# Two Fourier transforms and two feed-forward layers on one core: the start of the kernel rearranged, and the order in which a block leaves its accumulators

## The chip, the core and the metric

The kernel runs on one core of a Trainium2 chip. The time is the device time of one execution in microseconds; before the change it was 970.33 us, the median of three runs (968.51, 970.33 and 970.53 us). Engines are named as in the profile: PE (TensorE matmul) with PEld (its weight loads), DVE (VectorE), ACT (ScalarE), POOL (GpSimd) and SP, which issues nearly all transfers.

## The reference, cut to what matters

```
X = np.fft.fft(x, axis=1); X = np.fft.fft(X, axis=2); x = X.real.reshape(6016, 256)
h = x @ w_in;   g = np.maximum(h, 0) + alpha * np.minimum(h, 0);   x = g @ w_out     # 2048 wide
h = x @ w_in2;  g = h * (1 / (1 + np.exp(-h)));                    out = g @ w_out2  # 2048 wide
```

x is (2, 3008, 256) in f32. The weights arrive as 64-bit floating-point words and are narrowed to f32 on the chip.

## The kernel before, in words

The sequence of 3008 is taken as 47 times 64. Stage A transforms the 47, stage B the 64; the transform over the 256 features is not run on the data but multiplied into `w_in` once ("mixing", `mix_w`). The token columns are cut into NC = 6 blocks `c` of 8 rows by 64 columns, the 2048 hidden units into NF = 16 groups `m` of 128. Products that need f32 accuracy are made from a high part in a reduced f32 format and a low part (the rest): three matmuls of 512 columns stand for one.

**The front** (lines 887 to 993). `spin` issues ten dummy matmuls on zeros. The first image's x is loaded in eight pieces `x0`, of eight rows each, between raw weights (512 KB each); `stage_u` takes eight rows at a time, two matmul records a row, and ACT and DVE in turn copy the result into `u_all`. Between the units the first two input weights (`first[0]`, `first[1]`) and the first output weight (`wo0`) are narrowed and the first two are mixed. Then come stage B of block 0 (`psB`, line 976), one matmul that spreads a row over all partitions (`psP`, line 989) and its copies `pb` (991).

**First layer** (line 1030 on). Step (c, m) is `step1`: two groups of three matmuls into `psh` (line 578, three PSUM banks with tag "h"), then on DVE h (586), the sum (587) and the difference (589), on ACT two Relus (588, 590), on DVE two `r` (592). A bank is free for a later step when its `r` is done. `close1` splits r into `gh` (ACT, 608) and `gl` (POOL, 609) and queues `second1`: eight matmuls with gh and four with gl into four `pso` banks (624). It is pulled two steps later, eight in the first half of that step and four in the second. After the twelve matmuls of a block's last m, `save_x2` copies the four `pso` banks out, two on ACT (635) and two on DVE (636), and the next block uses the same four banks.

**Side work.** `at(step, job)` starts a job (a generator) at a step; it goes on at phases of the steps (`EARLY`, `BANK`, `AMID`, `MID1`, `MID2`, `LATE`). `win` narrows and mixes an input weight (ACT 227 and 228, DVE 233 and 235, PE 534, DVE 549 for the low part, then the `column` sums on PE, 540). `narrow_wout` narrows an output weight and ends with its high part on ACT (279) and its low part on POOL (280); pair n is first used by `second1(0, 2n)`. For the output weights with no raw tile of their own the load is issued at the named step and the narrowing follows two steps later. `back_stage_a` is stage A of the second image, `stage_b` the stage B of later blocks, four per block, and `rank_one(c)` computes a block's spread row, writes it to DRAM (480) and reads it back to all partitions as `pb[c]` (491). It waits for the four `stage_b` of its block; the read is issued two steps after the matmul. A block's first h (586) needs `pb[c]`. All steps are constants: `NARROW`, `WOUT`, `STAGE_A`, `STAGE_B`.

**Second layer** (line 1045 on). Same pattern with seven products per pair (744), sums (765) and second products (812); the change touches it in one line.

SP issues transfers in the order of the program and waits at each for the data it needs.

Of the kernel before, what the change touches and what calls it, by code (L numbers as in the profile page):

```python
# [97 lines left out]
def kernel(  # L98
# [422 lines left out]
    def mix_w(p, pool=None, tag="x"):  # L521
# [22 lines left out]

        if p < 2:

            column(pool.tile([P, 2, 2], F32, name="psS", tag=tag))
        yield BANK
        V.tensor_tensor(lo, ps, f32(hi), op=ALU.subtract)
        mixed.add(p)  # L550
        if p > 1:
            yield EARLY
            yield from claim()
            column(ptile([P, 2, 2], "psS"))

    def win(p, convert):
# [6 lines left out]
    def step1(c, m):  # L563
# [22 lines left out]
        V.scalar_tensor_tensor(t[:, :w], pb[c][:, :w], wst[:, m, 0:1], ps[0][:, :w], op0=ALU.mult, op1=ALU.add)  # L586
        V.tensor_tensor(ps[0][:, :w], t[:, :w], ps[1][:, :w], op=ALU.add)  # L587
        A.activation(r[:, 0, :w], ps[0][:, :w], AF.Relu, scale=-1.0)  # L588
        V.tensor_tensor(ps[1][:, :w], t[:, :w], ps[1][:, :w], op=ALU.subtract)  # L589
# [22 lines left out]
    def second1(c, m, hi, lo):  # L612
# [7 lines left out]
        for passes in (((0, hi), (1, hi)), ((0, lo),)):  # L620
            for s in range(2):
                for k in range(2):
                    for a, g in passes:
                        T.matmul(po[c][s][k][:, :w], wo1[q][:, mm, a, k * P:(k + 1) * P], g[:, s, :w],  # L624
                                 start=m == 0 and a == 0 and g is hi, stop=m == NF - 1 and g is lo)
                        n += 1
                        if n == 12 and m == NF - 1:
                            save_x2(c)
                        yield

    def save_x2(c):
# [217 lines left out]
    def start_win2():  # L849
# [20 lines left out]
    STEP2 = [0] + [NC * NF + 56 * c for c in range(NC - 1)]  # L870
    SPIN = 10,

    BEHIND = {2: ("i", 0), 4: ("i", 1), 7: ("o", 0)}
    UNITS = 8, 8, 8, 8, 8, 8, 8, 4, 4
    AMONG = {0: ((0, 1),), 1: ((0, 5),), 2: ((1, 1),), 3: ((1, 5),), 4: ((2, 1),), 8: ((2, 4),)}
    RAWS = {"o0": (0, "wA2"), "o1": (1, "wA2"), "i2": (0, "px1"), "i3": (1, "px1"), "i4": (0, "wA3"), "i5": (1, "wA3"),
            "o2": (0, "px2"), "o3": (1, "px2"), "i6": (0, "px6"), "i7": (1, "px6")}
    RAW_ORDER = ("i", 2), ("o", 1), ("i", 3), ("o", 2), ("i", 4), ("o", 3), ("i", 5), ("i", 6), ("i", 7)
    NARROW = 0, 2, 4, 6, 7, 8
    WOUT = 0, 1, 3, 5, 5, 7, 9, 11  # L880
    STAGE_A = 12, 17, 18, 19, 19, 21, 21, 22, 23, 25, 28, 27, 28, 29, 30, 30
    STAGE_B = (3, 6, 7, 9, 11), (16, 17, 18, 20, 23), (33, 36, 39, 40, 45), (43, 45, 46, 48, 51), (51, 53, 56, 60, 61)
    nx, ng = N2 // NX, CK // KG
    with tc.manual_schedule():
# [15 lines left out]
        ac = wtile([P, 2 * NP1], F32, "const", "h")  # L900
        nc.sync.dma_start(ac, a0)
        place_pq(0)
# [11 lines left out]
        for i in range(nx):  # L914
            if i % 2 == 0:
                t = keep.tile([P, 2, NX, P], F32, name="x0", tag=f"wo1_{i // 2}")
            xr.append(t[:, i % 2])
            for a, n in ((0, NX),) if i else ((0, NX // 2), (NX // 2, NX // 2)):
                nc.sync.dma_start(xr[i][:, a:a + n], x0[i, :, a:a + n])
            if i in BEHIND:  # L920
                kind, n = BEHIND[i]
                if kind == "i":
                    next(first[n])
                else:
                    load_raw(kind, n)
        A.dma_start(cwt.rearrange("p k e j -> p (k e j)"), cw)
        A.dma_start(cbts.rearrange("p a e k -> p (a e k)"), cb)
        con = wtile([2 * NP1, 192], F32, "const", "y")
# [5 lines left out]
        uv = u_all.rearrange("p c e k (t j) -> p (c e k) t j", t=2)  # L934
        done = 0

# [18 lines left out]
        for i, n in enumerate(UNITS):  # L955
            stage_u(n, i % 2)
            if i == 4:
                run(mix_w(0, pp, "o"))
            for g, k in AMONG.get(i, ()):
                for _ in range(k):  # L960
                    next(first[g] if g < 2 else wo0, 0)
        run(mix_w(1, pp, "o"))
        assert done == N2
# [3 lines left out]
        ur, cbt = u_all[:, 0], side(0)  # L967
        V.tensor_copy(cat.rearrange("p s m -> p (s m)"), con)
        row = wtile([P, CK, N2], F32, "row0", "h")
        G.tensor_tensor(row, ur[:, 1, :, 0:1].to_broadcast([P, CK, N2]),  # L970
                        cbt[:, 0:1].to_broadcast([P, CK, N2]), op=ALU.mult)
        for eo, h in ((0, 0), (0, 1), (1, 0), (1, 1)):
# [19 lines left out]
        A.activation(rest, ps[:, 0, OWN:K20], AF.Copy)  # L992
        V.tensor_scalar(al, al, -1.0, 1.0, op0=ALU.mult, op1=ALU.add)


        for p in range(2, 8):
            at(NARROW[p - 2], win, p, narrow_win(p, raws["i", p]))
        for n in range(1, 8):
# [46 lines left out]
        for n, (c, p) in enumerate(pairs):  # L1045
            length = len(CHUNKS[n])
            for j in range(length):
# [80 lines left out]
```

## Time and profile before

| what | value |
|---|---|
| median of three runs | 970.33 us |
| the profiled execution, and its span | 968.19 us, 966.4 us |
| DVE, ACT, POOL busy | 71%, 61%, 53% |
| HBM read and written | 33.28 MB, 13.51 MB |
| dummy matmuls, front, first layer, second layer | 1.3 to 5.7, to about 31, to about 484, to 966 us |

The execution's own time is 1.8 us more than the span from its first to its last instruction. PE is the engine with least idle time, so the profile is read for the places where PE waits, and for what it waits.

### The profile page before, as it was taken

The numbers are of one execution on the slowest core, as the hardware profiler recorded it, in microseconds if no ns is written. First come the engines' busy times: TensorE is split into PE (matmuls) and PEld (weight loads), VectorE is DVE, ScalarE is ACT, GpSimd is POOL, SyncE is SP. The second block draws the span as 40 slices with busy tenths as digits, with TensorE's granted clock in tenths as the row PEclk, the third lists the DMA queues.
The fourth block names the chain that finished last, engine by engine and source line by source line (L and its number), as shares of the span: only waits on it lengthen the run. The fifth ranks groups of instructions, "written<-read, shape, count | busy, mean of one in ns | idle before, by whom it ended". The sixth has DMA issues, their size and how long they took to land.

```text
span 966.4 us, 12441 instructions
## 1 busy us (share of the span) xinstructions
PE 946.5 (98%) x4374; PEld 792.6 (82%) x4374; DVE 689.8 (71%) x1070; ACT 593.9 (61%) x1010; POOL 507.7 (53%) x329
## 2 busy tenths in 40 slices
PE   9899899999999999999999999999999999999998
PEld 8789778877878877778799988888888888888886
DVE  4888677788888889878776765676576666557554
ACT  5776576665666556656776665665575565556554
POOL 0455577754545557978994633543354253334322
PEclk9999999999999999999999999999999999999999
DMA  9401122333333111020010020010010001001001
GB/s 343 158 10 50 28 60 65 94 99 119 100 127 104 38 39 45 12 66 12 22 55 12 1 82 1 1 44 0 1 45 1 1 1 44 1 1 45 1 1 43
DMA packets 30861, 47.58 MB, mean 49 GB/s; under 512 B 3312, under 2 KB 13392, under 8 KB 30544
## 3 DMA queue, kind: packets, MB, share of 16 engines
q1 hardware_dynamic: 30512, 46.41, 14.7%
q8 instruction: 34, 0.56, 0.2%
q10 hardware_dynamic: 288, 0.39, 0.1%
q14 instruction: 27, 0.22, 0.1%
HBM read 33.28 MB, written 13.51 MB: 48 GB/s over the span
## 4 chain that ended last, share of the span: by engine, by line
PE 85%; DVE 5%; POOL 4%; ACT 2%; issue 2%; DMA 1%; SPq 0%; ACTq 0%; POOLq 0%; DVEq 0%
PE pso L812 27%; PE psh L744 23%; PE pso L624 20%; PE psh L578 10%; DVE r L592 2%; POOL gl L609 2%; PE psB L416 1%; ACT r L588 1%; PE psW L534 1%; DVE psh L587 1%; PE psU L943 1%; DMA x<-in_x 1%; DVE x L636 1%; POOL wi L328 1%; DVE h L586 1%
## 5 line engine op out<-in xcount | busy, mean ns | idle before, releaser
L765 DVE TENSOR_TENSOR ring<-ring,psh 128x512 f32<-128x512 f32 (+1 forms) x336 | 222.1, 674 | 167.8 <-PE psh L744 158.6
L812 PE MATMUL pso<-ghl,wAo 128*128 128x512 f32 (+1 forms) x1152 | 309.8, 385 | 0.0
L609 POOL TENSOR_TENSOR gl<-r,gh 128x1024 fp32r<-128x1024 f32 (+1 forms) x96 | 226.2, 2357 | 141.9 <-ACT gh L608 89.0
L744 PE MATMUL psh<-ts,wi 128*128 128x512 f32 (+1 forms) x1008 | 279.0, 385 | 0.0
L756 POOL TENSOR_TENSOR ghl<-ring,ghl 128x512 fp32r<-128x512 f32 (+1 forms) x96 | 137.2, 1429 | 252.7 <-ACT ghl L751 172.6
L812 PEld LDWEIGHTS pso<-ghl,wAo 128*128 128x128 f32 x1152 | 216.2, 188 | 40.7
L768 ACT ACTIVATE ring<-ring 128x512 f32<-128x512 f32 (+1 forms) x192 | 119.3, 621 | 176.5 <-DVE ring L765 174.5
L744 PEld LDWEIGHTS psh<-ts,wi 128*128 128x128 f32 x1008 | 189.1, 188 | 35.5 <-DVE r L592 0.3
L624 PE MATMUL pso<-gh,wo_o 128*128 128x512 f32 (+1 forms) x768 | 188.3, 386 | 3.6 <-POOL wo_o L280 3.6
L578 PE MATMUL psh<-pq,wa 128*128 128x512 f32 (+1 forms) x576 | 165.6, 396 | 5.7 <-DVE r L592 5.7
L624 PEld LDWEIGHTS pso<-gh,wo_o 128*128 128x128 f32 x768 | 144.1, 188 | 31.8 <-POOL wo_o L280 4.7
L592 DVE SCALAR_TENSOR_TENSOR r<-r,al,psh 128x512 f32<-128x512 f32 (+1 forms) x192 | 134.0, 734 | 22.0 <-ACT r L588 11.7
L608 ACT ACTIVATE gh<-r 128x1024 fp32r<-128x1024 f32 (+1 forms) x96 | 100.3, 1045 | 69.5 <-DVE r L592 69.1
L578 PEld LDWEIGHTS psh<-pq,wa 128*128 128x128 f32 x576 | 105.0, 188 | 29.0 <-DVE r L592 10.2
L751 ACT ACTIVATE ghl<-ring 128x512 fp32r<-128x512 f32 (+1 forms) x192 | 119.0, 620 | 6.2
L624 PE MATMUL pso<-gl,wo_o 128*128 128x512 f32 (+1 forms) x384 | 102.3, 388 | 3.3 <-POOL gl L609 3.3
L588 ACT ACTIVATE r<-psh 128x512 f32<-128x512 f32 (+1 forms) x96 | 56.3, 587 | 74.3 <-DVE psh L587 71.5
L587 DVE TENSOR_TENSOR psh<-h,psh 128x512 f32<-128x512 f32 (+1 forms) x96 | 65.8, 685 | 49.8 <-PE psh L578 45.4
L624 PEld LDWEIGHTS pso<-gl,wo_o 128*128 128x128 f32 x384 | 71.8, 188 | 19.1 <-POOL gl L609 5.5
L756 DVE TENSOR_TENSOR ghl<-ring,ghl 128x512 fp32r<-128x512 f32 (+1 forms) x96 | 77.1, 803 | 4.0 <-ACT ghl L751 3.5
L586 DVE SCALAR_TENSOR_TENSOR h<-pb,wst,psh 128x512 f32<-128x512 f32 (+1 forms) x96 | 70.0, 729 | 0.7 <-ACT pb L991 0.7
L589 DVE TENSOR_TENSOR psh<-h,psh 128x512 f32<-128x512 f32 (+1 forms) x96 | 65.1, 679 | 0.0
(89 smaller groups left out, 634.8 us busy)
## 6 DMA issues: line engine op xcount, KB each, us to landing
raw<-in_w_in SPq DMA_DIRECT2D x16, 512.0 KB, 6.0
raw<-in_w_out SPq DMA_DIRECT2D x16, 512.0 KB, 7.2
out_dram<-ob SPq DMA_DIRECT2D x20, 256.0 KB, 2.1
x<-in_x SPq DMA_DIRECT2D x7, 512.0 KB, 9.8
xr<-in_x SPq DMA_DIRECT2D x16, 192.0 KB, 2.4
tmid<-ev SPq DMA_DIRECT2D x48, 64.0 KB, 1.8
ur<-tmid SPq DMA_DIRECT2D x12, 256.0 KB, 3.4
stash_o<-y SPq DMA_DIRECT2D x8, 256.0 KB, 2.2
```

Source lines behind the costliest of these rows:

```text
L578: T.matmul(t[:, :w], wa[q][:, mm, eo, a, :], pq[c][:, 2 * eo + bb, :w], start=n == 0, stop=n == 2)
L586: V.scalar_tensor_tensor(t[:, :w], pb[c][:, :w], wst[:, m, 0:1], ps[0][:, :w], op0=ALU.mult, op1=ALU.add)
L592: V.scalar_tensor_tensor(r[:, s, :w], r[:, s, :w], al[:, m:m + 1], ps[s][:, :w], op0=ALU.mult, op1=ALU.add)
L608: A.activation(hi[:, :, :w], r[:, :, :w], AF.Copy)
L609: G.tensor_tensor(lo[:, :, :w], r[:, :, :w], f32(hi[:, :, :w]), op=ALU.subtract)
L624: T.matmul(po[c][s][k][:, :w], wo1[q][:, mm, a, k * P:(k + 1) * P], g[:, s, :w], start=m == 0 and a == 0 and g is hi, stop=m == NF - 1 and ...
L744: T.matmul(bank[j][:, :w], wi2[p][:, FORMS[j], a], t[:, :w], start=a == 0 and t is hi, stop=t is lo)
L751: A.activation(outs[p, i][:, 0, :w], g[:, :w], AF.Copy)
L756: eng.tensor_tensor(hl[:, 1, :w], g[:, :w], f32(hl[:, 0, :w]), op=ALU.subtract)
L765: V.tensor_tensor(dst[:, :w], a[:, :w], bank[j][:, :w], op=ALU.add)
L768: A.activation(a[:, :w], a[:, :w], AF.Silu)
L812: T.matmul(po[c, 2][s][k][:, :w], wo2[q][:, mm + m, a, k * P:(k + 1) * P], outs[p, i][:, g, :w], start=p == 0 and i < 2 and a == 0 and g == 0,
```

## The change

1. The dummy matmuls go from ten to six (`SPIN`). The constant `ac` is issued from ACT's queue. Of x, the first piece is loaded as two, two and four rows, the second as four and four (`HEAD`); the constants `cw` and `cb` leave ACT's queue for SP's, behind the fifth and the last piece of x. The first two raw input weights are loaded one piece of x later each, and behind the last piece comes the third input weight in place of the first output weight (`BEHIND`, `RAWS`, `RAW_ORDER`).
2. The third input weight is narrowed between the units of the front (`AMONG`) and mixed in the middle of step 0 (`early_mix`). The first output weight is narrowed during stage B of block 0. The column sums of weight 1 move to step 0, and weight 0's and 1's low parts are taken a little later.
3. The `psP` matmul and its copies move ahead of the second half of block 0's stage B; `al` is computed earlier.
4. New start steps: input weights 3 to 7 at 1, 3, 5, 7, 7 (they were 2, 4, 6, 7, 8), output weights 1 to 7 at 0, 2, 4, 4, 6, 7, 10 (1, 3, 5, 5, 7, 9, 11), and new lists for `STAGE_A` and `STAGE_B`.
5. `save_x2(c)` is no longer called where the twelfth matmul is issued. It is put on a list and called in the same step behind the sum (587).

```diff
-        if p < 2:
+        if p == 0:
             column(pool.tile([P, 2, 2], F32, name="psS", tag=tag))
         yield BANK
         V.tensor_tensor(lo, ps, f32(hi), op=ALU.subtract)
         mixed.add(p)
+        if p == 1:
+            yield EARLY
+            yield MID1
+            column(pso.tile([P, 2, 2], F32, name="psS", tag="o"))
...
+    def early_mix():
+        yield MID1
+        taken.add(1)
+        yield from mix_w(2, psh, "x")
...
         V.tensor_tensor(ps[0][:, :w], t[:, :w], ps[1][:, :w], op=ALU.add)
+        save_due()
...
                         if n == 12 and m == NF - 1:
-                            save_x2(c)
+                            due.append(c)
...
+    def save_due():
+        while due:
+            save_x2(due.pop())
...
-    SPIN = 10,
-    BEHIND = {2: ("i", 0), 4: ("i", 1), 7: ("o", 0)}
+    SPIN = 6,
+    BEHIND = {3: ("i", 0), 5: ("i", 1), 7: ("i", 2)}
+    HEAD = {0: ((0, 2), (2, 2), (4, 4)), 1: ((0, 4), (4, 4))}
-    AMONG = {0: ((0, 1),), 1: ((0, 5),), 2: ((1, 1),), 3: ((1, 5),), 4: ((2, 1),), 8: ((2, 4),)}
+    AMONG = {0: ((0, 1),), 1: ((0, 5),), 2: ((1, 1),), 3: ((1, 5),), 4: ((2, 1),), 6: ((2, 9),)}
-    NARROW = 0, 2, 4, 6, 7, 8
-    WOUT = 0, 1, 3, 5, 5, 7, 9, 11
-    STAGE_A = 12, 17, 18, 19, 19, 21, 21, 22, 23, 25, 28, 27, 28, 29, 30, 30
-    STAGE_B = (3, 6, 7, 9, 11), (16, 17, 18, 20, 23), (33, 36, 39, 40, 45), (43, 45, 46, 48, 51), (51, 53, 56, 60, 61)
+    NARROW = 1, 3, 5, 7, 7
+    WOUT = 0, 0, 2, 4, 4, 6, 7, 10
+    STAGE_A = 12, 19, 17, 19, 23, 14, 21, 29, 32, 19, 27, 29, 35, 32, 29, 34
+    STAGE_B = (5, 5, 6, 12, 6), (15, 12, 4, 21, 30), (28, 33, 43, 42, 33), (45, 55, 36, 50, 43), (49, 46, 53, 57, 62)
...
-        nc.sync.dma_start(ac, a0)
+        A.dma_start(ac, a0)
...
-            for a, n in ((0, NX),) if i else ((0, NX // 2), (NX // 2, NX // 2)):
+            for a, n in HEAD.get(i, ((0, NX),)):
...
-        A.dma_start(cwt.rearrange("p k e j -> p (k e j)"), cw)
-        A.dma_start(cbts.rearrange("p a e k -> p (a e k)"), cb)
+            if i == 4:
+                nc.sync.dma_start(cwt.rearrange("p k e j -> p (k e j)"), cw)
+        first.append(narrow_win(2, raws["i", 2]))
+        nc.sync.dma_start(cbts.rearrange("p a e k -> p (a e k)"), cb)
...
-        run(mix_w(1, pp, "o"))
+        w1 = mix_w(1, pp, "o")
+        next(w1)
+        next(w1)
...
-            if eo == 0 and h:
-                run(wo0)
-        ps = pso.tile([P, CK, N2], F32, name="psP", tag="o")
-        T.matmul(ps, ones[:, 0:1].to_broadcast([P, P]), row, start=True, stop=True)
-        for dst, src in spread(0, lambda k0, k1, w: ps[:, k0:k1, :w]):
-            A.activation(dst.rearrange("p (k c) -> p k c", c=src.shape[2]), src, AF.Copy)
+            if (eo, h) == (0, 1):
+                pc = pso.tile([P, CK, N2], F32, name="psP", tag="o")
+                T.matmul(pc, ones[:, 0:1].to_broadcast([P, P]), row, start=True, stop=True)
+                for _ in range(4):
+                    next(wo0)
+            if (eo, h) == (1, 0):
+                for dst, src in spread(0, lambda k0, k1, w: pc[:, k0:k1, :w]):
+                    A.activation(dst.rearrange("p (k c) -> p k c", c=src.shape[2]), src, AF.Copy)
+        run(wo0)
...
+        at(0, lambda: w1)
+        at(0, early_mix)
...
                 pull(CHUNKS[n][j])
+                save_due()
```

## Rows read from the trace of the kernel before

**Rows 1.** The page, part 1: busy us of each engine, share, instructions.

```profile
PE 946.5 (98%) x4374; PEld 792.6 (82%) x4374; DVE 689.8 (71%) x1070; ACT 593.9 (61%) x1010; POOL 507.7 (53%) x329
```

**Rows 2.** Waits of PE, whole span: us in total, times, longest.

```profile
PE psh L578 <- DVE r L592: 5.7, 7, 1.7
PE pso L624 <- POOL wo_o L280: 3.6, 3, 1.7
PE pso L624 <- POOL gl L609: 3.3, 5, 0.9
...
PE psU L943 <- DMA x<-in_x: 0.2, 1, 0.2
```

**Rows 3.** Waits of PE, the first 50 us.

```profile
PE psh L578 <- DVE r L592: 1.7, 1, 1.7
...
PE pso L624 <- POOL wo_o L280: 0.5, 1, 0.5
```

**Rows 4.** Waits of PE in 90-116, 116-200, 200-365 and 365-485 us, one each.

```profile
PE pso L624 <- POOL wo_o L280: 3.1, 2, 1.7
...
PE psh L578 <- DVE r L592: 0.3, 1, 0.3
...
PE psh L578 <- DVE r L592: 2.5, 4, 1.3
...
PE psh L578 <- DVE r L592: 1.2, 1, 1.2
```

**Rows 5.** Timeline, PE, front: start, us, instructions; in brackets its wait.

```profile
1.31 4.64 PE L897 MATMUL idle<-zero 128*128 128x512 f32 x10 [1.31 <-POOL zero L888]
5.75 6.31 PE L943 MATMUL psU<-const,x 128*128 128x96 f32 x48
12.24 3.78 PE L943 MATMUL psU<-const,x 128*128 128x96 f32 x32 [0.18 <-DMA x<-in_x]
...
25.15 0.50 PE L540 MATMUL psS<-ones,wq 128*128 128x2 f32 x4
...
35.30 1.97 PE L534 MATMUL psW<-wq,cwt 128*128 128x256 f32 x8 [0.75 <-DVE wq L235]
```

**Rows 6.** Windows of 4 us: busy time by engine, granted PE clock, DMA share, GB/s.

```profile
8.00:12.00 4.00, 4.00 (x35) 3.77 (x34) 1.66 (x3) 3.09 (x6) 0.00 (x0) 1.00 1.03 408
```

**Rows 7.** Timeline, ACT, front.

```profile
20.34 0.67 ACT L227 ACTIVATE y<-raw 128x512 f32<-128x512 f32 x1 [1.62 <-DMA raw<-in_w_out]
...
21.81 3.31 ACT L951 ACTIVATE u_all<-psU 64x384 f32<-64x384 f32 x8 [0.24 <-PE psU L943]
```

**Rows 8.** Timeline, DVE, steps 0 to 2.

```profile
34.47 0.69 DVE L235 CUSTOM_DVE_ANT_0 wq<-raw,wq 128x1024 uint16<-128x1024 uint16 x1
...
39.28 0.68 DVE L549 TENSOR_TENSOR wa<-psW,wa 128x512 fp32r<-128x512 f32 x1
```

**Rows 9.** Timeline, 92 to 100 us, POOL: stage A's low part, the output weight's.

```profile
96.08 1.29 POOL L365 TENSOR_TENSOR xhl<-xr,xhl 96x512 fp32r<-96x512 f32 x1 [1.52 <-ACT xhl L361]
...
99.55 1.26 POOL L280 TENSOR_TENSOR wo_o<-y,wo_o 128x512 fp32r<-128x512 f32 x1
```

**Rows 10.** Timeline, 340 to 352 us, where block 3 ends.

```profile
343.43 1.07 PE L624 MATMUL pso<-gl,wo_o 128*128 128x512 f32 x4
...
344.08 1.29 DVE L636 COPY x<-pso 128x512 f32<-128x512 f32 x2 [1.70 <-PE pso L624]
...
345.01 1.97 PE L624 MATMUL pso<-gh,wo_o 128*128 128x512 f32 x8
345.29 0.74 DVE L586 SCALAR_TENSOR_TENSOR h<-pb,wst,psh 128x512 f32<-128x512 f32 x1
...
348.28 0.96 PE L578 MATMUL psh<-pq,wa 128*128 128x512 f32 x3 [1.29 <-DVE r L592]
```

**Rows 11.** Line 491, reads of the spread row: issue to landing.

```profile
DMA to landing us min/median/max: 3.7/4.6/5.6
```

**Rows 12.** Timeline, SP, 90 to 130 us: four issues merged.

```profile
105.31 23.60 SPq L356 DMA_DIRECT2D xr<-in_x  x4
```

More of the change, by code (lines that the diff above doesn't have):

```diff
@@ L627, in second1 @@
                         if n == 12 and m == NF - 1:
-                            save_x2(c)
+                            due.append(c)
                         yield
+    due = []
+    def save_due():
+        while due:
+            save_x2(due.pop())
     def save_x2(c):
@@ L870 @@
     STEP2 = [0] + [NC * NF + 56 * c for c in range(NC - 1)]
-    SPIN = 10,
-    BEHIND = {2: ("i", 0), 4: ("i", 1), 7: ("o", 0)}
+    SPIN = 6,
+    BEHIND = {3: ("i", 0), 5: ("i", 1), 7: ("i", 2)}
+    HEAD = {0: ((0, 2), (2, 2), (4, 4)), 1: ((0, 4), (4, 4))}
     UNITS = 8, 8, 8, 8, 8, 8, 8, 4, 4
-    AMONG = {0: ((0, 1),), 1: ((0, 5),), 2: ((1, 1),), 3: ((1, 5),), 4: ((2, 1),), 8: ((2, 4),)}
-    RAWS = {"o0": (0, "wA2"), "o1": (1, "wA2"), "i2": (0, "px1"), "i3": (1, "px1"), "i4": (0, "wA3"), "i5": (1, "wA3"),
+    AMONG = {0: ((0, 1),), 1: ((0, 5),), 2: ((1, 1),), 3: ((1, 5),), 4: ((2, 1),), 6: ((2, 9),)}
+    RAWS = {"o0": (0, "wA2"), "o1": (1, "wA2"), "i2": (0, "wo1_1"), "i3": (1, "wo1_1"), "i4": (0, "wA3"), "i5": (1, "wA3"),
             "o2": (0, "px2"), "o3": (1, "px2"), "i6": (0, "px6"), "i7": (1, "px6")}
-    RAW_ORDER = ("i", 2), ("o", 1), ("i", 3), ("o", 2), ("i", 4), ("o", 3), ("i", 5), ("i", 6), ("i", 7)
-    NARROW = 0, 2, 4, 6, 7, 8
-    WOUT = 0, 1, 3, 5, 5, 7, 9, 11
-    STAGE_A = 12, 17, 18, 19, 19, 21, 21, 22, 23, 25, 28, 27, 28, 29, 30, 30
-    STAGE_B = (3, 6, 7, 9, 11), (16, 17, 18, 20, 23), (33, 36, 39, 40, 45), (43, 45, 46, 48, 51), (51, 53, 56, 60, 61)
+    RAW_ORDER = ("o", 0), ("o", 1), ("i", 3), ("o", 2), ("i", 4), ("o", 3), ("i", 5), ("i", 6), ("i", 7)
+    NARROW = 1, 3, 5, 7, 7
+    WOUT = 0, 0, 2, 4, 4, 6, 7, 10
+    STAGE_A = 12, 19, 17, 19, 23, 14, 21, 29, 32, 19, 27, 29, 35, 32, 29, 34
+    STAGE_B = (5, 5, 6, 12, 6), (15, 12, 4, 21, 30), (28, 33, 43, 42, 33), (45, 55, 36, 50, 43), (49, 46, 53, 57, 62)
     nx, ng = N2 // NX, CK // KG
@@ L921 @@
                 kind, n = BEHIND[i]
-                if kind == "i":
+                if kind == "i" and n < 2:
                     next(first[n])
@@ L934 @@
         uv = u_all.rearrange("p c e k (t j) -> p (c e k) t j", t=2)
-        done = 0
+        done, mixes = 0, []
         def stage_u(n, on_v):
@@ L957 @@
             if i == 4:
-                run(mix_w(0, pp, "o"))
+                mixes.append(mix_w(0, pp, "o"))
+                next(mixes[0])
+            if i == 5:
+                run(mixes[0])
             for g, k in AMONG.get(i, ()):
                 for _ in range(k):
-                    next(first[g] if g < 2 else wo0, 0)
-        run(mix_w(1, pp, "o"))
+                    next(first[g], 0)
+        w1 = mix_w(1, pp, "o")
+        next(w1)
+        next(w1)
         assert done == N2
@@ L968 @@
         V.tensor_copy(cat.rearrange("p s m -> p (s m)"), con)
+        V.tensor_scalar(al, al, -1.0, 1.0, op0=ALU.mult, op1=ALU.add)
         row = wtile([P, CK, N2], F32, "row0", "h")
@@ L985 @@
                 V.tensor_tensor(lo, src, f32(hi), op=ALU.subtract)
-            if eo == 0 and h:
-                run(wo0)
-        ps = pso.tile([P, CK, N2], F32, name="psP", tag="o")
-        T.matmul(ps, ones[:, 0:1].to_broadcast([P, P]), row, start=True, stop=True)
-        for dst, src in spread(0, lambda k0, k1, w: ps[:, k0:k1, :w]):
-            A.activation(dst.rearrange("p (k c) -> p k c", c=src.shape[2]), src, AF.Copy)
[L992 to L997, printed above, removed]
+            if (eo, h) == (0, 1):
[7 more added lines that the diff above has]
+        run(wo0)
+        A.activation(rest, pc[:, 0, OWN:K20], AF.Copy)
+        at(0, lambda: w1)
+        at(0, early_mix)
+        for p in range(3, 8):
+            at(NARROW[p - 3], win, p, narrow_win(p, raws["i", p]))
         for n in range(1, 8):
```

## The prediction

> **What bounds the kernel now.** The busy shares come first: PE is busy 946.5 of 966.4 us and no other engine comes near [rows 1]. So the time is PE's work plus PE's idle time, 19.9 us, and only the second and the pace of the dummy matmuls can be changed here: the change leaves all other matmuls as they are. The waits of PE come next, since they say what the idle time is made of [rows 2]: 5.7 us before `psh` for a bank that `r` on DVE still holds, 3.6 us before `pso` for the low part of an output weight on POOL, 3.3 us for `gl` on POOL. The same view by windows says where. Of the first kind 1.7 us are one wait in step 0 [rows 3], and 0.3 + 2.5 + 1.2 = 4.0 us are six waits between 116 and 485 us [rows 4]; the timeline of the longest shows that it stands at a block's end [rows 10]. Of the second kind 0.5 us stand in the first steps [rows 3] and 3.1 us, in two waits, between 90 and 116 us [rows 4]. The timeline of the front then shows what precedes step 0: the dummy matmuls, 64 rows of x and two mixings, with almost no gap [rows 5].
>
> **The front.** The ten dummy matmuls take 4.44 us to the first x matmul (5.75 less 1.31), 0.44 us each; the 32 later x records take 3.78 us, 0.118 us each, and the first 48 take 6.31 us where 48 times 0.118 is 5.66 [rows 5]. So the first few x records ran slowly: 0.65 us too much is five or six of them at double time. 512 columns in 0.44 us is the pace of the 1.2 GHz level, and after these x records the pace is that of the 2.4 GHz level, which a granted clock of 1.00 stands for from 8 us on [rows 6]. Four dummies fewer let x start 4 x 0.44 = 1.76 us earlier. If PE stays busy and the clock rises at the moment it did before, those 1.76 us are worked at half pace: 1.76 / 0.236 is 7.5 records, which at full pace are worth 0.88 us. The 0.18 us wait for x goes too, since x no longer stands behind a weight there [rows 5]. Together 1.05 us. The column sums of weight 1 (0.50 us as a record, some 0.34 us of PE's time) leave the front as well, for step 0, where PE waits anyway.
>
> Is x there in time? The first piece is now 128 KB behind 48 KB on the other queue; at 408 GB/s, the rate once transfers flow [rows 6], a 512 KB piece takes 1.29 us, and PE needs 16 x 0.118 = 1.9 us for it. So x comes faster than PE uses it, and the smaller first pieces only have to be there at the start. The weights, not x, are what comes late: ACT waits 1.62 us for the raw output weight behind x, and its eight `u_all` copies end at 25.12 us [rows 7], 0.5 us before the column sums do (25.65, [rows 5]) and stage B of block 0 begins. The third input weight takes that place, behind nearly the same number of bytes; ACT narrows it there (two passes) before its last copies. So ACT gets to these copies hardly earlier than before, PE reaches stage B of block 0 about 1.05 us earlier instead of 1.4, and the 0.34 us of the column sums are lost at this point. Bounds for the whole front: 0.3 us (x or the weight late) to 1.4 us.
>
> `psP` ahead of the second half of stage B: the same PE work in another order. `pb` is ready earlier, but the sum (587) also needs the low parts of the second half, which now end about 0.9 us later relative to the end of `psP`. I take nothing, with 0.3 us either way.
>
> **Steps 0 to 2.** PE idles 1.7 us for the bank in step 0 [rows 3] and 0.75 us before mixing weight 2 [rows 5], which waits for its narrowing on DVE. Now weight 2 is already narrow and its eight mixing matmuls (1.75 us of PE) and the column sums lie in the first of these gaps. DVE loses the narrowing of weight 2 but has the low part of the mixed weight (0.68 us) a step earlier [rows 8], and output weight 1 comes at step 0 in the place of weight 2, with a pass like the 0.69 us one [rows 8]. So DVE's first steps hold as much as before, less the little that went into the front, and the third `psh` bank is late next: I put a new wait of 1.2 to 1.4 us before the second half of step 2. Of the 2.4 us I take 0.75 as won; bounds 0 and 2.4.
>
> **Output weights.** In the first wait at 99 us, POOL has first a low part of stage A (1.29 us), then `gl`, then the weight's low part (1.26 us, from 99.55) [rows 9], while PE stands ready. The new list moves output weights 4 to 7 forward by one step, one, two, one; a step with twelve `pso` and six `psh` matmuls is some 4 us, more than either wait (the longest 1.7 us [rows 4]). The two waits go, 3.1 us. What would be late next is `gl` itself, which POOL can do in time when the weight is out of its way. Input weights 3 to 7 come a step earlier as well (6 not), so DVE's load moves but does not grow. The 0.5 us in the first steps I leave inside the term before. I take 3.1; bounds 1.5 (new crowding in steps 4 to 10) and 3.6, all waits of this kind [rows 2].
>
> **The block's copies.** In the row group of block 3, PE ends `gl` at 344.50, DVE copies two banks from 344.08 for 1.29 us, and only then begins h, 345.29, though the bank for h was full long before: DVE had been idle 1.70 us in front of the copies [rows 10]. h, sum, difference, Relu and `r` follow, and PE waits 1.29 us at 348.28 for that `r`. With the copies behind the sum, h uses the idle time, the sum can run when its own three matmuls end (just before `gl`), and the copies lie where DVE waits for ACT's Relu. `r` is earlier by the 1.3 us of the copies and about 0.1 to 0.3 us more: as much as the longest wait. What is late next would be the copies: the next block's eight matmuls begin at 345.01 and need the first DVE bank two matmuls later, near 345.5, the second four later, near 346.5. The sum's matmuls end as `gl` begins, 343.43, so it would end near 344.2 and the copies near 344.85 and 345.5. That fits. All five block ends with a wait have this form. I take 3.5 of the 4.0 us; bounds 1.5 and 4.0.
>
> **Spread rows.** `rank_one` for blocks 1, 2 and 3 can now end only in the last two steps before the block: `STAGE_B` places the last part of block 1 at 12 (done in 13), the row's matmul in 14, and its read in 16, the block's first step; block 2 has matmul 30 and read 32, block 3 about 46 and 48. The read takes 3.7 to 5.6 us to land [rows 11] and waits on SP behind the previous step's saves. I work out that it lands some 4 to 5 us into the block's first step, where h would want it at 2. `r` of that step is used only in the second half of the next step, some 7.5 us in, and h, sum, difference, Relu and `r` take 2.7 us from the landing. So the slack is near nothing: cost 0 to 2.5 us in all, 0.3 taken.
>
> The rest (`al`, later stage A steps, the third kind of wait, which stands at 366 us and later with unchanged code, the last 4 us) I leave at nothing, 1 us either way.
>
> **Sum.** 1.05 + 0.75 + 3.1 + 3.5 - 0.3 = 8.1 us. The profiled execution took 968.19 us (span 966.4 and 1.8 around it), so it would take 960.1. That execution and one of three runs (968.51) lie some 2 us under the other two (970.33, 970.53), so I take the middle, 969.4, less 8.1: **961.3 us**.
>
> **Rivals.** (a) *The copies only move the wait.* The banks come free too late for the next block and PE waits before `pso` instead of `psh`. For it: the same four banks are reused within half a microsecond. Against it: the times above. It takes back 3.5 us: 964.8. (b) *The clock rises later.* If x is not there when six dummies end (3.95 us), PE has a gap and may stay at the lower level for longer. I price it as two pieces of x, 32 records, at half pace: 26.5 more than before, 3.1 us, less the 1.76 us of the earlier start, leaves 1.4 us lost where 0.9 were won: 963.6. The Trainium skill (TensorE: Matmul & The Clock Gate, What's actually happening) has the array's clock at half rate by default and released by recent activity, not by a number of matmuls, which speaks against taking dummies away; the slow dummies in this trace agree with the half rate at the start, at 0.44 us each, and nothing here shows a gap's price. For the rival: the transfers start slowly. Against: the first piece is half as big as before, and nothing stands before it on SP. (c) *Slower: a spread row stuck on SP.* SP issues in order, and four x loads held it for 23.60 us [rows 12]. If the read of `pb` for blocks 1 to 3 stands behind a load or save that waits a step more, it lands one step (4.8 us) later, beyond the slack: 3 x 4.8 = 14.4 us lost against 8.4 won is 6 us slower, 975. It decides when the read is issued more than about 2.7 us into the block's first step. Against it: the save ahead of it belongs to the step before. (d) *The side work is not moved enough*: the lists crowd steps 4 to 12, and steps and output weights give 1.5 in place of 3.85: 963.7.
>
> **Chances.** Forecast (6.5 to 10 us won) 0.55; (a) 0.1; (b) 0.1; (d) or a late row of 1 to 3 us, 0.13; (c) 0.06; nothing won because several lists cost elsewhere 0.06. What a measurement can tell from no change is 0.2%, 1.9 us, as the three runs spread by 2.0. Faster 0.87, same 0.07, slower 0.06. The range: all terms at their good ends are 1.4 + 2.4 + 3.6 + 4.0 = 11.4 us, which is not likely at once; I go to 958.0. Upward it holds (a), (b) and (d) and stops at 967.0.
>
> **What would show it.** Right: x matmuls from about 4 us and stage B of block 0 a little over 1 us earlier; mixing of weight 2 in step 0's gap; no wait for `wo_o` near 100 us; no wait for `r` where h follows a block's end; DVE copies between sum and difference. Wrong: a `pso` matmul that waits for the copies, x records at double time for longer, h waiting for a transfer in steps 16, 32 or 48, new waits for POOL in steps 4 to 12, or PE's busy time changed by more than the dummies' 2 us. The forecast fails above all if new waits there eat what the old ones give.

## The result, and the profile after

The changed kernel takes 956.44 us, the median of four runs (955.97 to 956.55), beside 969.66 us for the kernel before (968.51 to 970.53; the three runs known before and one of 968.99): ratio 0.9863, 95% interval 0.9846 to 0.9881. So 13.2 us were won where 8.1 were forecast, and the time lies below the range (958.0). The profiled executions differ by 11.8 us (956.42 against 968.19, spans 954.6 and 966.4), and this is the difference that the rows can explain. The first part of the page after:

```profile
PE 941.5 (99%) x4370; PEld 792.1 (83%) x4370; DVE 691.3 (72%) x1070; ACT 592.9 (62%) x1010; POOL 508.2 (53%) x329
```

PE's idle time went from 19.9 to 13.1 us, and its busy time fell by 5.0 us [rows 1], of which the dummies are 1.7 (2.93 us for six records where ten took 4.64). Waits of PE after, whole span (us in total, times, longest):

```profile
PE pso L634 <- POOL gl L619: 2.9, 5, 0.8
PE idle L914 <- POOL zero L905: 1.3, 1, 1.3
PE psB L1001 <- ACT u_all L970: 1.1, 1, 1.1
PE psU L962 <- DMA x<-in_x: 1.1, 2, 0.9
PE psS L540 <- DVE pq L435: 0.8, 1, 0.8
PE psW L534 <- ACT wst L541: 0.8, 1, 0.8
PE psh L587 <- DVE r L602: 0.7, 1, 0.7
```

Beside [rows 2] the wait for `wo_o` is gone (3.6) and that for `r` is down from 5.7 to 0.7; that for `gl` is as it was; waits for x (0.2 before) and for `pq` (0.4 before) have grown, those for `u_all` and `wst` are new. The timeline of PE, after, up to step 1:

```profile
1.31 2.93 PE L914 MATMUL idle<-zero 128*128 128x512 f32 x6 [1.31 <-POOL zero L905]
4.04 3.25 PE L962 MATMUL psU<-const,x 128*128 128x96 f32 x24
8.15 5.08 PE L962 MATMUL psU<-const,x 128*128 128x96 f32 x40 [0.86 <-DMA x<-in_x]
...
25.81 2.00 PE L1001 MATMUL psB<-cbt,u_all 128*128 128x64 f32 x16 [1.07 <-ACT u_all L970]
...
32.05 1.97 PE L534 MATMUL psW<-wq,cwt 128*128 128x256 f32 x8
...
35.93 1.89 PE L634 MATMUL pso<-gh,wo_o 128*128 128x450 f32 x8
...
38.82 0.88 PE L587 MATMUL psh<-pq,wa 128*128 128x450 f32 x3 [0.67 <-DVE r L602]
39.54 0.98 PE L634 MATMUL pso<-gl,wo_o 128*128 128x450 f32 x4
41.31 1.99 PE L534 MATMUL psW<-wq,cwt 128*128 128x256 f32 x8 [0.80 <-ACT wst L541]
```

x starts 1.71 us earlier than in [rows 5], then PE waits 0.86 us for x, and again before stage B of block 0. ACT's timeline says why the second: it stands 0.75 us for the raw third weight ahead of its eight `u_all` copies.

```profile
21.30 0.68 ACT L227 ACTIVATE wq<-raw 128x512 f32<-128x512 f32 x1 [0.75 <-DMA raw<-in_w_in]
21.88 0.68 ACT L228 ACTIVATE raw<-raw 128x512 int32<-128x512 uint32 x1
22.45 3.31 ACT L970 ACTIVATE u_all<-psU 64x384 f32<-64x384 f32 x8
```

Weight 2 is mixed in step 0 without a wait (32.05). The first matmul with gh comes at 35.93 us; before it was at 37.72. Where block 3 ends (timeline of all engines, after; beside [rows 10]):

```profile
333.89 0.74 DVE L595 SCALAR_TENSOR_TENSOR h<-pb,wst,psh 128x512 f32<-128x512 f32 x1
...
335.06 1.07 PE L634 MATMUL pso<-gl,wo_o 128*128 128x512 f32 x4
...
335.25 0.70 DVE L596 TENSOR_TENSOR psh<-h,psh 128x512 f32<-128x512 f32 x1 [0.63 <-PE psh L587]
335.48 1.09 ACT L651 ACTIVATE x<-pso 128x512 f32<-128x512 f32 x2 [0.41 <-PE pso L634]
...
335.86 1.28 DVE L652 COPY x<-pso 128x512 f32<-128x512 f32 x2
...
336.64 1.98 PE L634 MATMUL pso<-gh,wo_o 128*128 128x512 f32 x8
337.06 0.69 DVE L599 TENSOR_TENSOR psh<-h,psh 128x512 f32<-128x512 f32 x1
...
338.76 0.97 PE L587 MATMUL psh<-pq,wa 128*128 128x512 f32 x3
```

h lies before the `gl` matmuls, the sum beside them, the copies between sum and difference; the next block's eight matmuls start without a wait.

**A ledger by steps.** A step runs from one start of eight gh matmuls to the next. From its length I subtract the side work in it (mixing 1.75 us, a `psB` group 0.84, a `psA` group 0.70, column sums 0.36, a row's matmul 0.17) and the length of a step without side work and without a wait (4.08 us; in block 0 3.72 and 3.88). What is left is the step's excess, in us (steps counted from the first gh; the kernel's own count is two higher, and some of the expectations below use that one):

| | before | after |
|---|---|---|
| steps 0 to 9 | 2.2 | 3.5 |
| steps 12, 14 (waits for the output weight) | 3.66 | 0.04 |
| steps 16, 32, 48, 49, 64, 80 (a block's end) | 6.00 | 0.55 |
| steps 39, 44, 46 | 1.5 | 0.2 |
| steps 71, 74, 76, 79, 92 (waits for `gl`) | 5.0 | 4.8 |

So of the 11.8 us, 1.8 come before the first gh, but step 11 begins only 0.28 us earlier (94.69 against 94.97): steps 0 to 9 give the rest back. 3.6 are output weights, 5.45 block ends, 0.4 lie behind step 96. What remains, about 2 us, is left for the new lists; 1.3 of it stand in steps 39, 44 and 46. The 3.5 us of steps 0 to 9 do not depend on when these steps begin: no_copies, big_pieces, swap_places, spin10_new and late_passes (below) have the same steps, their first gh lies between 35.23 and 39.73 us, and their excess there is 3.4 to 3.5 us each.

### The profile page after: what moved, and what is told of

It reads as the page before. It is cut to its first block, busy times and chain, and to the rows that moved or that the text cites. A ratio compares the mean times of both kernels' runs of the same rounds, so it can differ in the third digit from the quotient of the medians.

```text
span 954.6 us, 12440 instructions
## 1 busy us (share of the span) xinstructions
PE 941.5 (99%) x4370; PEld 792.1 (83%) x4370; DVE 691.3 (72%) x1070; ACT 592.9 (62%) x1010; POOL 508.2 (53%) x329
## 4 chain that ended last, share of the span: by engine, by line
PE 88%; POOL 4%; DVE 3%; ACT 2%; DMA 1%; issue 1%; SPq 0%; POOLq 0%; ACTq 0%; DVEq 0%
PE pso L828 27%; PE psh L760 24%; PE pso L634 22%; PE psh L587 11%; POOL gl L619 2%; PE psB L416 2%; DVE r L602 1%; DMA raw<-in_w_in 1%; POOL wi L328 1%; DMA x<-in_x 1%; ACT r L598 1%; DVE psh L596 1%; PE psW L534 1%; PE psU L962 0%; PE psA L371 0%
```

## The experiments

Each kernel has runs of the kernel before beside it on the same chip; the medians of these are 968.2 to 969.3 us. "Old" is as in the kernel before. Differences are between medians. "Above after" is a difference from 956.44 us; the kernel before took 969.66 us beside that, so by the medians of the kernel before such a difference is good to about 1 us.

**Old copies in the new kernel (no_copies), the new copies alone in the old one (copies_only).**

```diff
 # no_copies
-                            due.append(c)
+                            save_x2(c)
```

> The changed kernel with part 5 taken back: the copies are issued at the twelfth matmul again. Theory 1: 5.5 us slower than the changed kernel, some 962. Theory 2: 3.5 to 4.0 slower, some 960. If the parts help one another (less than either because the new lists alone leave DVE free at a block's end): under 3.

> The kernel before with part 5 alone: a block's copies behind the next step's sum, everything else as before. Theory 1 (a stall costs what its step is longer than an undisturbed one of 4.08 us, side work taken off; over the five block ends 0.66 + 0.88 + 0.75 + 0.56 + 1.59 + 1.56 = 6.0 us before, 0.5 us after): 5.5 us faster than before, each of these steps back at 4.1 to 4.5 us. Theory 2 (a stall costs what the wait rows of PE say, 4.0 us, as the prediction had it): 3.5 to 4.0 us faster. If steps 38 and 39 (226 to 237 us, 1.75 us too long together, no wait of that size in the rows) become normal too, that loss hung on the copies as well.

no_copies: 961.33 us, 0.9923 (0.9898 to 0.9947), 4.9 above after; its block ends have excesses of 0.61, 0.89, 0.68, 1.59 and 1.56 again. copies_only: 962.51, 0.9935 (0.9911 to 0.996), 5.7 below its before, excess 0.7 over all block ends. Part 5 is worth 4.9 us in the new kernel and 5.7 in the old one, more than the 4.0 us of wait rows. The row itself shows why. PE's timeline of no_copies, steps around the end of block 3, one with the wait and one without:

```profile
341.86 0.96 PE L587 MATMUL psh<-pq,wa 128*128 128x512 f32 x3 [1.29 <-DVE r L602]
342.66 1.08 PE L634 MATMUL pso<-gl,wo_o 128*128 128x512 f32 x4
...
344.25 1.98 PE L634 MATMUL pso<-gh,wo_o 128*128 128x512 f32 x8
346.07 0.84 PE L587 MATMUL psh<-pq,wa 128*128 128x512 f32 x3
346.75 1.07 PE L634 MATMUL pso<-gl,wo_o 128*128 128x512 f32 x4
```

Undisturbed, `psh` starts 1.82 us after the eight gh matmuls (346.07 less 344.25), though their record lasts 1.98: records overlap by 0.16 us. The wait is counted from the record's end, so it starts 0.16 us late; and after a wait the next group starts 0.80 us on, not 0.68, another 0.12. A wait row of 1.29 us is a loss of 1.57, and the 0.28 us between stand in PE's busy time: eight waits fewer at block ends and output weights are 2.2 of the 3.3 us by which it fell beside the dummies. Six rows of 4.0 us in all then mean 4.0 + 6 x 0.28 = 5.7, near the 6.0 of the ledger. In the same way 0.3 us without any row are lost in after, at 338.76 (2.12 us after 336.64).

**Old output-weight steps (old_wout), old stage lists (old_stages).**

```diff
 # old_wout
-    WOUT = 0, 0, 2, 4, 4, 6, 7, 10
+    WOUT = 0, 1, 3, 5, 5, 7, 9, 11
```

> The changed kernel with the list WOUT of before (output weights 2 to 7 one or two steps later again). Theory 1 (the price is the step's excess): steps 12 and 14 are long again by 1.7 and 2.0 us, 3.7 us slower than the changed kernel, with perhaps 0.7 us more or less in steps 2 to 5. Theory 2 (the price is the wait rows): 3.1 us slower. Theory 3: other lists (stage A's first piece is no longer in step 13) took the crowding away and WOUT does nothing: 0.

> The changed kernel with the lists STAGE_A and STAGE_B of before. Theory 1: the 1.75 us lost in steps 38 and 39 and some 0.7 us in steps 44 to 46, which the changed kernel no longer loses, come from these lists: 2 to 2.5 us slower than the changed kernel, and these steps are long again. Theory 2: they hung on the copies or on when the weights come: no slower, the steps normal.

old_wout: 965.01 us, 0.9971 (0.995 to 0.9993), 8.6 above after, where 3.6 was the price by the ledger. Not steps 12 and 14 alone came back (1.5 and 0.5); steps 2, 4 and 6 grew to 1.7, 2.0 and 3.4. Waits of PE in old_wout:

```profile
PE pso L634 <- POOL wo_o L280: 3.1, 4, 1.4
...
PE psS L540 <- DVE pq L435: 3.0, 2, 1.5
PE psB L1001 <- ACT u_all L970: 2.0, 1, 2.0
```

The longest wait for `wo_o`, 1.4 us, is one in step 2, so output weight 1 is late where the changed kernel has it in time; the other new waits are column sums that wait for the low parts `pq` on DVE. (The row for `psB` lies ahead of the first step, where old_wout is as after: executions with that front read 0.6 to 2.0 us there.) From 76 to 84 us the clock is down too (0.70 and 0.87). The mean clock of its ten executions is 0.989 to 0.998, where after has 0.999 and 1.000; 0.002 to 0.003 of 965 us, an estimate from these means, are 2 to 3 of the 8.6 us. Which of them follows from which I did not settle. old_stages: 959.23, 0.9901 (0.9875 to 0.9926), 2.8 above after: excess 1.0, 1.3, 0.8 and 0.3 in steps 6, 8, 39 and 44, where after has 0.4, 0.1, 0 and 0.1 (its 1.1 in step 4 is gone; step 2 has 0.45). The stage lists, which I priced at nothing, carry 2.8 us by the medians, 2.0 by the profiled executions (958.42 against 956.42).

**Old front, new rest (old_front).** Weights 2 and 3 are narrowed in steps 0 and 1 (NARROW 0, 1, 3, 5, 7, 7), since the front no longer does weight 2.

> The front of the kernel before (ten dummies, order of the loads, weight 2 narrowed in step 0, psP at the end) with the copies, WOUT, STAGE_A and STAGE_B of the changed one; input weights 2 to 7 at 0, 1, 3, 5, 7, 7. Theory 1 (the new front wins next to nothing: the changed kernel reaches its twelfth second-layer product only 0.3 us earlier than the kernel before): within 1 us of the changed kernel, 956 to 957.5 on a chip where that takes 956.4. Theory 2 (the prediction's 1.8 us for front and first steps were won and lost again elsewhere): 1.8 us slower or more.

964.28 us, 0.9951 (0.9934 to 0.9968), 7.8 above after. PE's timeline in step 0, then the windows (us of the window, busy us by engine, granted clock, DMA share, GB/s):

```profile
34.25 0.88 PE L578 MATMUL psh<-pq,wa 128*128 128x450 f32 x3 [2.32 <-DVE r L593]
36.21 3.75 PE L534 MATMUL psW<-wq,cwt 128*128 128x256 f32 x8 [1.08 <-DVE wq L235]
39.40 1.69 PE L578 MATMUL psh<-pq,wa 128*128 128x450 f32 x3
40.88 2.23 PE L625 MATMUL pso<-gh,wo_o 128*128 128x450 f32 x8
```

```profile
32.00:36.00 4.00, 0.88 (x3) 0.49 (x3) 3.25 (x8) 2.42 (x5) 0.00 (x0) 0.87 0.47 171
36.00:40.00 4.00, 3.79 (x9) 3.07 (x10) 3.51 (x7) 3.07 (x7) 3.34 (x2) 0.50 0.02 4
40.00:44.00 4.00, 4.00 (x17) 3.62 (x17) 2.78 (x6) 2.69 (x4) 2.14 (x1) 0.77 0.01 4
```

The bank is late by 2.32 us instead of 1.7, PE is busy 0.88 of 4 us, and the granted clock falls to 0.50, the 1.2 GHz level: mixing takes 3.75 us where it took 1.97. The first gh comes at 40.88, 3.2 us later than before, and steps 3 to 11 have 5.9 us of excess where before has 1.5. The mean clock of its four executions is 0.996 to 0.998, so some 2 of the 7.8 us are the clock, by the same estimate as for old_wout.

**The front alone (front_only), copies and output weights (copies_wout), front and copies (front_copies).**

> The new front (parts 1 to 3) alone: copies, WOUT, STAGE_A and STAGE_B as before, input weights 3 to 7 at 2, 4, 6, 7, 8 as before. Theory 1 (the front wins nothing by itself: its 1.05 us went to a late weight 2 and to the crowding of ACT and DVE in steps 1 and 2): first second-layer product 1.5 to 2 us earlier than before, steps 2 to 8 give it back; 0 to 1.5 us slower than before, as the changed kernel with the old WOUT lost 8.6 us. Theory 2 (the prediction: 1.8 us for front and first steps): 1.5 to 2 us faster than before.

> The kernel before with the copies behind the sum and with output weights 5 to 7 at 6, 7, 10 instead of 7, 9, 11; front and all else as before. Theory 1 (the prices are step excesses and the parts add: 5.4 for the copies, 3.7 for the two waits on POOL): 9 us faster than before, steps 14 and 16 at their floor. Theory 2 (the lists only work with the new front, as the old front with all new lists took 7.8 us more than the changed kernel): 5.7 us as the copies alone, or less, with new excess in steps 7 to 12.

> The new front and the copies behind the sum together, with the old start steps of input weights, output weights and both stages (input weights 3 to 7 at 2, 4, 6, 7, 8). Theory 1 (the front wins nothing by itself, and the copies are worth 5 to 5.7 us by themselves, whatever stands around them): as much as the copies alone, 962 to 963.5 us beside a kernel before of 968.8; the waits for wo_o of 4.1 us in the run with the front alone stay. Theory 2 (front and copies help each other, as front and lists do): 960 us or less.

front_only: 967.7 us, 0.9994 (0.9984 to 1.0004): no difference that can be told (the medians are 1.1 us apart). Its first gh comes at 34.95, 2.8 us earlier than before; at step 11 the lead is 0.7 (94.28). copies_wout, with output weights 5 to 7 at 6, 7, 10: 963.28, 0.9935 (0.992 to 0.995), no more than the copies alone. Steps 12 and 14 do lose their 3.6 us, but steps 7 and 9 have 1.45 and 3.45 us of excess where the kernel before has 0.3 each. In 92 to 96 us, within step 9, the granted clock is 0.59, so a part of that step's excess is the clock. Its waits of PE:

```profile
PE psS L540 <- DVE pq L435: 3.0, 3, 1.5
PE psh L578 <- DVE r L593: 1.7, 1, 1.7
```

front_copies: 963.29, 0.9943 (0.993 to 0.9957), again the copies alone (4.4 us below front_only). So the front, and the steps of output weights 5 to 7, each without the rest, win nothing that can be told from no change; the whole list of output weights and the stage lists were not run by themselves. Together the three win what is left beside the copies, 13.2 - 5.7 = 7.5 us (no_copies, which has them without the copies, lies 6.9 below its kernel before). Taking the stage lists, the output weights or the front back costs 2.8, 8.6 or 7.8.

**Inside the front (big_pieces, swap_places, spin10_new, late_passes).** x in the old first pieces; the third weight's raw tile in a place free from the start (`wA2`); ten dummies; the third weight narrowed two units later.

```diff
 # big_pieces
-    HEAD = {0: ((0, 2), (2, 2), (4, 4)), 1: ((0, 4), (4, 4))}
+    HEAD = {0: ((0, 4), (4, 4))}
 # spin10_new
-    SPIN = 6,
+    SPIN = 10,
 # late_passes
-    AMONG = {..., 4: ((2, 1),), 6: ((2, 9),)}
+    AMONG = {..., 8: ((2, 9),)}
```

> The changed kernel with x cut as before (first piece in two halves of 256 KB, the others whole). Theory 1 (small pieces cost rate: 193 to 234 GB/s between 4 and 7 us against 240 to 385 before, some 0.4 MB behind at 7 us, so the third piece of x came 0.86 us late): the rate is back above 300, that wait is gone or under 0.3 us, the weights come 0.5 to 1 us earlier; the first x matmul is later by up to 0.7 us. In all -0.5 to +0.3 us. Theory 2 (the rate is set by the order, not by the size): the wait of 0.86 us stays.

> The changed kernel with the raw tiles exchanged: weight 2 (and 3) in the place wA2, the output weights 0 and 1 in wo1_1, where pieces 2 and 3 of x lie. Theory 1 (SP holds the load of weight 2 from about 10 to 13.27 us because its place is still being read as x): the load is issued near 10 us, the weight lands 0.5 to 1 us earlier than at 21.2, ACT's 0.75 us wait and most of PE's 1.07 us before stage B go; 0.5 to 1 us faster. Theory 2 (transfers are full from 5 us on, so it lands when its bytes have their turn): lands at the same time within 0.3 us, same time.

> The kernel after with ten dummy matmuls instead of six. Theory 1 (the four dummies are worth about 0.9 us at the x units, as forecast, but x units are not what the first step waits for, so the time stays): 956 to 957 us; the wait before stage B of block 0 (1.1 us) shrinks by what the front starts later. Theory 2 (they lie wholly on the path): 957.3 us or more, with that wait as long as before.

> The changed kernel with ACT's two passes for weight 2 behind the last u_all copies instead of between them, and DVE's behind these. Theory 1 (PE's 1.07 us before stage B of block 0 is a wait for ACT, which waits in order for the late weight and only then copies): that wait goes, stage B of block 0 begins about 1 us earlier; up to 1 us faster, if weight 2 is mixed in step 0 without a wait. Theory 2 (DVE and ACT set step 0 anyway): the wait moves to the bank for step 0's mixing or to the first sum; same within 0.4 us.

big_pieces: 958.23 us, 0.9888 (0.9863 to 0.9913). From 4 to 8 us its transfers run at 344 GB/s where after shows 240, no matmul waits for x, and stage B of block 0 begins at 24.95 us instead of 25.81. That much is within scatter: the other executions with the front of after (front_only, old_stages, no_copies, front_copies, old_wout) begin it between 25.05 and 27.19. Then, in the profiled execution, the clock goes:

```profile
28.00:32.00 4.00, 4.00 (x19) 3.81 (x18) 1.53 (x4) 1.74 (x7) 0.00 (x0) 0.50 1.05 386
32.00:36.00 4.00, 4.00 (x19) 3.60 (x17) 2.98 (x6) 2.96 (x8) 1.29 (x1) 0.74 0.58 215
```

Of its four executions three have a mean clock of 0.996 or 0.997 and take 957.7 to 960.0 us; the one with 1.000 takes 956.7, as long as after. swap_places: 956.32, 0.9868 (0.9852 to 0.9885), as after. SP issues the weight's load at 11.09 us instead of 13.27, but ACT still waits for the weight, until 21.64 us (21.30 in after), and PE's wait for `u_all` is 1.0 us, much as theory 2 had it. spin10_new: 956.68, 0.9885 (0.9868 to 0.9903), as after too, so the four dummies alone win nothing. Both theories had the wait before stage B of block 0 wrong: it was 1.73 us in the profiled execution, though 0.6 to 2.0 us occur with six dummies as well (old_stages, old_wout). That execution took 960.44 us, with the clock at 0.63 and 0.52 in 28 to 36 us; the other three, with 0.999 or 1.000, took 956.22 to 956.73. late_passes: 955.5 (955.26 to 956.2), 0.9862 (0.9845 to 0.9879). With ACT's narrowing behind the copies stage B begins at 24.11 us, 1.7 earlier (24.03 to 24.96 in the five kernels built on it), but `psP` then waits 0.8 us for `wa` and the first gh is 0.7 earlier (35.23). It is the fastest version run, 0.1% below after, less than can be told from no change.

**On top of late_passes (late_narrow, late_stageb, late_host_pool).** Weight 3 at step 2 instead of 1; block 1's `STAGE_B` at 7, 8, 11, 12; and, for the waits for `gl`, POOL's part of the second layer's work (`SE`) given to DVE, with the small copy at a block's end moved from ACT to DVE.

> late_passes with input weight 3 started at step 2 instead of 1. Theory 1 (the 2.0 us that step 2 of the changed kernel is too long come from ACT and DVE holding two weights in step 1: 0.67 us wait for r, 0.8 us for the bank before the mixing): that step is back within 0.5 us of 3.72, up to 1.5 us faster than late_passes. Theory 2 (the work only moves a step): the excess appears one step later; same within 0.4 us.

> late_passes with the parts of block 1's stage B at 7, 8, 11, 12 instead of 5, 5, 6, 12. Theory 1 (the 1.1 to 1.3 us that step 6 of the changed kernel is too long are the column sums waiting for DVE to empty the same bank after a stage B part in the same step): that excess goes, 1.0 to 1.3 us faster than late_passes. Theory 2 (it moves with the parts): appears at the new steps; same, or slower where four parts crowd the steps just before block 1.

> late_passes with two further edits of a line each: block 3's extra copy of two columns on DVE instead of ACT, and the four small sums that narrow_win2 makes on POOL moved to DVE. Theory 1 (step 66's excess of 0.45 us is ACT waiting for DVE's copies in front of the Relu; and the excess of 0.5 + 1.2 + 1.0 + 0.9 + 1.1 us in steps 73 to 94 is POOL, which has 1.9 us of these sums per weight beside 2.4 us of gl per step): 0.4 us and 2 to 4 us faster than late_passes, some 951 to 953. Theory 2 (DVE, 86% busy there, becomes what is late): the waits for gl become waits for r; same or slower.

960.52 us (0.9918, 0.9905 to 0.9932), 957.76 (0.989, 0.9876 to 0.9903) and 966.82 (0.9981, 0.9972 to 0.999): all slower than late_passes. late_narrow was to free step 1; step 0 of the ledger went from 2.0 us of excess to 1.0, as theory 1 had it, but steps 1, 3, 5, 7 and 11 got 1.8, 1.5, 1.1, 1.4 and 1.3. late_stageb takes step 4's excess from 1.1 to 0.3 and puts 1.5 and 1.3 into steps 6 and 8. In late_host_pool the waits for `gl` are gone and DVE is late in their stead, and the mean clock is 0.994 to 0.996:

```profile
PE psh L587 <- DVE r L602: 9.7, 6, 4.5
```

**Two more near late_passes (late_swap_host, late_after_w1).** The small copy at a block's end on DVE, `SE` as it was; with the third weight's tile in the free place, or with all its passes behind those of weight 1.

> late_passes with the raw tiles exchanged (weight 2 in wA2) and block 3's extra copy of two columns on DVE. Theory 1: the copy's 0.45 us in step 66 go (ACT no longer waits for DVE ahead of the Relu), and the earlier weight lets DVE begin before the last copies: 0.4 to 0.9 us faster than late_passes, 954.6 to 955.1. Theory 2 (the 0.45 us are DVE's copies themselves): as late_passes.

> late_passes with weight 2's passes behind the low part of weight 1, and block 3's extra copy on DVE. Theory 1 (the 0.82 us that PE waits before psP in late_passes are DVE narrowing weight 2 ahead of weight 1's low part, which holds the bank): that wait goes, 0.8 + 0.4 us faster than late_passes, 954.3. Theory 2 (ACT is full there): stage B of block 0 waits for ACT's high parts instead, and weight 2's mixing in step 0 waits; same or slower.

956.79 (0.9872, 0.9857 to 0.9887) and 955.79 us (0.9863, 0.9848 to 0.9877): neither beats late_passes. The small copy is no gain on DVE: the step that it was to shorten (64 of the ledger) has 0.64 and 0.61 us of excess where late_passes has 0.44. In late_after_w1 the wait before `psP` is gone, as theory 1 had it, but the first gh is only 0.14 us earlier (35.09).

**The clock in the old kernel (fill_step0).** Eight matmuls whose result nobody reads fill step 0's pause in the kernel before.

> The kernel before with eight extra matmuls of 448 columns (results unused) in the middle of step 0, where PE pauses 1.7 us and then 0.75 us. Theory 1 (the runs of before differ by 2 to 5 us because that pause sometimes lets TensorE's clock fall: its runs with a mean granted clock of 1.000 took 967.3 to 968.0, those of 0.998 and less up to 972.9): with the pause filled every run shows a clock of 0.999 to 1.000, all runs within 1 us, median near 967.7, 0.5 to 2 us faster than before. Theory 2 (the spread comes from the transfers or another state): spread and clock as before, and the same time or up to 0.5 us slower for the added matmuls.

968.37 us, 1.0 (0.9991 to 1.001), mean clock 0.998 to 1.000, but the spread stays at 2.4 us. So the spread of the old kernel's runs isn't the clock in that pause alone; what else it is stays open.

## Why the prediction was wrong

From the 8.1 us forecast to the 11.8 between the profiled executions, by the ledger: the copies +1.95, the output weights +0.5, spread rows +0.3, what is left for the stage lists +2.05, behind step 96 +0.4, the front and the first steps -1.5. The other 1.4 us to 13.2 are the median of the kernel before, which lies above its profiled execution.

- **The block's copies, "3.5 of the 4.0 us; bounds 1.5 and 4.0": the mechanism held, the size failed.** Everything that was said of order and slack is in the timeline after. It measured 5.45 us by the ledger, 4.9 and 5.7 by the runs. The upper bound was the sum of the wait rows, and each of the six hides 0.28 us: the bound should have been 5.7. The trace before had it: the step that begins at 345.01 [rows 10] lasts 5.67 us and the next 4.08, 1.59 us for a row of 1.29. So "PE's work plus PE's idle time", of which only the second can change, was wrong as a starting point too: beside the dummies 3.3 us of PE's busy time went.
- **"The rest ... at nothing, 1 us either way": failed.** Taking back the lists of both stages costs 2.8 us (old_stages), of which 0.8 and 0.3 in steps 39 and 44, where I looked for no cost at all.
- **Output weights, 3.1: the two waits went, as forecast.** They are 3.6 by the ledger, two rows of 3.1 with twice 0.28. That this is a gain by itself did not hold (copies_wout, and the next point but one).
- **The front, 1.05, and steps 0 to 2, 0.75: failed as terms.** The first gh is 1.8 us earlier, but step 11 only 0.28. That the clock rises at the moment it did before did not hold for the profiled pair, and not because of the change: the moment differs from execution to execution. In after the x records go from 0.21 us apart to 0.11 at about 4.5 us, in the kernel before at about 7.0. swap_places, with the same six dummies and no wait among its first 24 x records, keeps the half pace until about 7.2, and takes 4.33 us for them where after takes 3.25:

```profile
4.03 4.33 PE L962 MATMUL psU<-const,x 128*128 128x96 f32 x24
```

  With ten dummies it came at 4.3 us (old_front), 5.1 (spin10_new) and 7.0 (before): the number of dummies doesn't set it. The Trainium skill's rule, a release by activity and not by a number of matmuls, agrees with that (TensorE: Matmul & The Clock Gate, What's actually happening). The saving of 0.88 us did not reach the end, as spin10_new with its ten dummies takes as long: PE waits for x and `u_all` instead, as "x or the weight late" had it at 0.3 us. What the first gh does gain, steps 0 to 9 take back for the most part by waits of their own (3.5 us of excess against 2.2).
- **The sum of separate terms: failed.** Front, output weights and lists have no prices that add. The front and part of the output weights alone win nothing that can be told, all three together 7.5 us. By PE's wait rows DVE's and ACT's work is what comes late in the first steps, and a job moved to an earlier step can make that step late (copies_wout: 3.6 us won in steps 12 and 14, 4.9 of excess in 7 and 9, which had 0.6). How much of this is the clock, which fell in copies_wout, old_wout and old_front, is open. Beside the copies 4.6 us were forecast (8.1 less 3.5).
- **Rivals.** (a) fell: no `pso` matmul waits for the copies. (b) fell in after: x was there when the six dummies ended. A pause followed by 4 us or more at the lower level did come in the neighbours, at another place: 1.1 to 2.3 us before stage B or in step 0 (big_pieces, spin10_new, old_front). (c) fell: no wait of PE for a spread row; the term of 0.3 is 0. The sign named for it did show once: h of block 2 waited for its row, and the steps around it (28 to 32) have no excess over 0.1 us, so the slack held.

```profile
DVE h L595 <- DMA pb<-rd: 2.2, 1, 2.2
```

  (d) fell for the change as it is; it is what front_only and copies_wout show.
- **The range** left out "all terms at their good ends" (11.4 us) as unlikely. With the copies' end at 5.7 these ends make 13.1, and 13.2 was measured against the runs' median. That the two nearly meet is chance: front and first steps gave 0.28 of their 3.8 us.

Not settled: why the clock fell in some executions of big_pieces and spin10_new and in none of after, whose wait before stage B is as long (1.07 against 1.12 us).

## What to carry to other kernels

Here a wait row of PE was a lower bound of its stall: compare the length of the step that holds it with the same step elsewhere, and the excess is the price. Jobs placed in the same few steps have no separate prices, so forecast them as one schedule and give the sum a range as wide as the whole. A front that starts earlier wins only what the first steps do not take back in waits of their own. And one profiled execution does not price an edit at the start of the kernel, where the clock's rise and the wait for x differ between executions of the same code.

## What the runs showed of the hardware

- Two TensorE groups overlap by 0.16 us in the records, and the first group behind a wait takes 0.12 us longer, so a row of 1.29 us is 1.57 us of time.
- After a pause of 1.1 to 2.3 us the granted clock went to 0.50 in old_front and big_pieces and to 0.52 in spin10_new, whose execution with the fall took 3.7 to 4.2 us longer than its others. After a pause of 1.07 us (after), 1.28 (front_copies), 1.36 (no_copies) or 2.0 us (old_wout) before stage B it did not fall there, nor after 1.66 us in step 0 of the kernel before. So the length of the one pause doesn't decide it.
- The granted clock reads 1.00 between 3 and 4 us, where a dummy takes 0.44 us; three matmuls of as many columns take 0.68 later. That column doesn't show the slow start; the pace of equal matmuls does. By that pace the clock rose between 4.3 us (old_front) and 7.2 us (swap_places). The window of after:

```profile
3.00:4.00 1.00, 1.00 (x3) 0.73 (x3) 0.00 (x0) 0.00 (x0) 0.00 (x0) 1.00 1.00 355
```

- Smaller first pieces of x went with fewer bytes between 4 and 8 us: 240 (after) to 324 GB/s in fourteen profiled executions, 326 to 359 in the six with larger pieces. Only big_pieces (344) differs from after in the pieces alone; the others of the six have the old order of loads too.
